# First batch's second attention stage: tokens on the PSUM partitions and PE transposes, in place of packed queries on the partitions and VectorE transposes

## The chip, the cores and the metric

The kernel runs on one core of a Trainium2 chip. The metric is the device time of one execution in microseconds (us), the median of several runs. A profiled execution of the kernel before is at hand: its span, its instructions by engine (PE is TensorE's matmuls, PEld its weight loads, DVE is VectorE, ACT is ScalarE, SP is SyncE, which issues most DMAs) and what each of them waited for.

## The reference: what is computed

Eight batches, eight heads of 64, 576 tokens. A set of 32 "packed" queries per head first attends to the tokens, and the tokens then attend to the 32 packed rows. An ELU feed-forward layer of width 2048 follows.

```
def sm_attn(qq, kk, vv):
    s = scale * np.matmul(qq, kk.transpose(0, 1, 3, 2))
    s = s - np.max(s, axis=-1, keepdims=True)
    a = np.exp(s)
    a = a / (np.sum(a, axis=-1, keepdims=True) + 1e-09)
    return np.matmul(a, vv)
p_packed = sm_attn(p, k, v)
out = sm_attn(q, p_packed, p_packed)
...
x = np.ascontiguousarray(attn_out.transpose(0, 2, 1, 3)).reshape(B * S, H * D)
h = x @ w_in
g = np.where(h > 0.0, h, alpha * (np.exp(np.minimum(h, 0.0)) - 1.0))
return (g @ w_out).astype(np.float32)
```

The weights arrive as 64-bit floats and are turned into 32-bit words on the chip.

## The kernel before, in words

**Stages.** For every batch, `attention` first lets the 32 packed queries of each head attend to all tokens: scores (`s1`, L476), maximum (`smax1`, L486), exponential (`sexp1`, L500), PE transposes of the exponentials (`tr1`, L531), the product with the values (`pv`, L557), its scaling by the sums (`norm`, L569), one more transpose (`tr2`, L583) and a copy that leaves the packed rows, heads stacked, in `ppT`. `mstep` multiplies these rows by w_in (L705), so that the up-projection later contracts over the 256 (head, packed row) pairs instead of 512 columns; its result `m_hi` is copied out by ScalarE. In the second stage the tokens attend to the packed rows: the scores of one half of the tokens (288) are made with the packed rows on the PSUM partitions (`s2`, L602: four heads' 32 rows in four strips of 32 partitions, two banks). The softmax runs over the 32 packed rows, so VectorE turns 32x32 blocks (`fold`, L610, one for each bank), and then takes the maximum (L617), the difference (L620), the sum (L630), the reciprocal (L633, L636) and the product (L639) along the free axis; ScalarE does the exponential (L626). VectorE turns the blocks back (`unfold`, L652) into `st.af`, where again the packed rows are on the partitions. For batches 0 and 1 the first quarter of the feed-forward layer reads `st.af` itself (L815, fp32); elsewhere a high and a low half are read (`a_hi` by a copy, `a_lo`, L658; L822).

**Feed-forward.** Each step of the order is a batch, a window of 256 or 320 of its tokens, and one of 16 blocks of the hidden width: up-projection (L815 or L822), relu and exponential on ScalarE (L829, L835), the ELU on VectorE (L838), and the down-projection (L932 fp32 for the first four blocks of batches 0 and 1, else L938, L939, L941). The first visits are batch 0's first window with blocks 0 to 3, its second window with the same blocks, then batch 1's.

**Weights.** `weights` turns each 128-wide block of w_in and w_out from 64-bit words into fp32 by four VectorE passes (L280, L295, L301, L308), a fifth that multiplies (L318) and two ScalarE passes (L287, L292). For w_out a high part (ScalarE, helper line L252) and a low part (VectorE, L331) are made beside.

**What sets the order.** A planner, `schedule`, takes all operations of the program with a priority and a planned cost for each engine and writes them out one by one. Each engine then works through its own list in that order: what stands behind a waiting instruction waits too. `T_ATT1`, `T_S2` and the like are priorities (a smaller one goes first), and a PSUM or SBUF buffer is given to an operation only when the planner sees it free. `temp()` hands batch 0 five buffers of its own.

Of the kernel before, what the change touches and what calls it, by code (L numbers as in the profile page):

```python
# [9 lines left out]
F32 = mybir.dt.float32  # L10
# [10 lines left out]
def packed_attention_elu_ffn(  # L21
# [58 lines left out]
    TM = [24.5, 24.5, 28.0, 28.0]  # L80
    T_S2, STAY, SWITCH = 0, 4, 0.12

    F_PLAIN, H_PLAIN = 4, [0, 1]
    T_WS, T_AS = 20, 6

# [160 lines left out]
    def ring_tile(ring, pool, shape, dt, tag, **kw):  # L248
        return Buf(R[ring], lambda: pool.tile(shape, dt, tag=tag, name=tag, **kw))
# [12 lines left out]
    def weights(f, first, prio):  # L262
# [71 lines left out]

        ld = op(-60 + f if first and f < 4 else -44 + f / 9 if f < 2 else prio - 8, {"DMA": 1.45}, load, take=[raw])
        x = op(prio, {"DVE": 0.42}, exponent, [ld], take=[ex_b], use=[raw])
# [32 lines left out]
    def attention(b, ts):  # L369

        st, prev_b = Batch(), sts.get(b - 1)
        p_b = ring_tile("p", small, [P, NPAIR, NPK], F32, "p")

# [15 lines left out]

        whole = b in H_PLAIN  # L390
        if whole:
# [18 lines left out]
        def queries(pair, half):  # L410
            if b == 0:
                return q_b[0].t[:, pair, half * HS:(half + 1) * HS]
            return q_b[half].t[:, :NPAIR * HS].rearrange("p (c s) -> p c s", c=NPAIR)[:, pair, :]

        def values(c, h):
# [30 lines left out]
        def load_q(e, n):  # L446
            if b == 0:
                nc.sync.dma_start(out=q_b[0].t, in_=qT[b])
            else:
                nc.sync.dma_start(  # L450
                    out=q_b[n].t[:, :NPAIR * HS].rearrange("p (c s) -> p c s", c=NPAIR),
                    in_=qT[b, :, :, n * HS:(n + 1) * HS],
                )

        lds, prev_ld = {}, prev_b and prev_b.ld_q
        for name, fn, bufs, t in (
            ("k", load_k, k_b, ts[0] - 6), ("v", load_v, v_b, ts[0] - 5), ("q", load_q, q_b, ts[0] - 3),
        ):
            lds[name] = []
            for n, x in enumerate(bufs):  # L460
# [130 lines left out]
        st.ppT_op = op(ts[3], {"ACT": 0.27, "DVE": 0.29}, tr2c, [o], use=[pt2, st.ppT])  # L591
        st.a_done, st.af_done = [], []
        prev = []
        for half in range(2):
            ps = banks(2)
# [19 lines left out]
            def smax(e, t3=t3, mx=mx):  # L615
                mx["t"] = small.tile([P, NB], F32, tag="mx2", name="mx2")
                nc.vector.tensor_reduce(out=mx["t"], in_=t3(), axis=AX.X, op=ALU.max)  # L617
# [10 lines left out]
            def ssum(e, t3=t3, sm=sm):  # L628
                sm["t"] = small.tile([P, NB], F32, tag="sm2", name="sm2")
                nc.vector.tensor_reduce(out=sm["t"], in_=t3(), axis=AX.X, op=ALU.add)  # L630
# [52 lines left out]
            )  # L683
            st.a_done.append(op(t, {"DVE": 0.75}, lo, [h], use=[t2, st.a]))
        st.tmp_last = prev[0]
        st.m, st.m_done = {}, {}
# [109 lines left out]
    for i, (b, win, f) in enumerate(order):  # L796
# [77 lines left out]
        a_b, a_done = (st.af, st.af_done) if h_whole else (st.a, st.a_done)  # L874
        need_a = a_done[0 if (b % 2, win) == (0, 0) else 1]
        cost = (1.07 if long else 0.87) if h_whole else (0.885 if long else 0.714)
# [138 lines left out]
```

## Time and profile before

| | |
|---|---|
| median of 3 runs | 725.19 us (724.35 to 727.75) |
| the profiled execution's own time | 724.5 us |
| its span | 722.3 us, so 2.2 us lie around it |
| PE matmuls, busy | 699.6 us, 97% |
| DVE, busy | 504.4 us, 70% |
| ACT, busy | 387.4 us, 54% |
| granted PE clock, mean | 0.998 |

Busy shares are averages over the whole span; the stage around the change is the first 40 us. A row of the chain of waits gives a start, a length and what ran; only the time by which a step moves the chain on is counted, so a step that overlaps its follower is shorter there than in the timeline, where each instruction has its full duration. One fp32 matmul of the program shows as two MATMUL rows. A matmul's shape gives the contraction and weight columns (64*32) and the moving operand (64x288).

### The profile page before, as it was taken

The numbers are of one execution on the slowest core, as the hardware profiler recorded it, in microseconds if no ns is written. First come the engines' busy times: TensorE is split into PE (matmuls) and PEld (weight loads), VectorE is DVE, ScalarE is ACT, GpSimd is POOL, SyncE is SP. The second block draws the span as 40 slices with busy tenths as digits, with TensorE's granted clock in tenths as the row PEclk, the third lists the DMA queues.
The fourth block names the chain that finished last, engine by engine and source line by source line (L and its number), as shares of the span: only waits on it lengthen the run. The fifth ranks groups of instructions, "written<-read, shape, count | busy, mean of one in ns | idle before, by whom it ended". The sixth has DMA issues, their size and how long they took to land.

```text
span 722.3 us, 13401 instructions
## 1 busy us (share of the span) xinstructions
PE 699.6 (97%) x5076; PEld 557.1 (77%) x5076; DVE 504.4 (70%) x1256; ACT 387.4 (54%) x900; POOL 19.4 (3%) x27
## 2 busy tenths in 40 slices
PE   2799999999999999999999999999999999999997
PEld 1454588887778877888878887888888877888886
DVE  6999998886875587545875569555686559654453
ACT  5777888885654455434454445434454345444332
POOL 0000002110111000000000000000000000000000
PEclk9999999999999999999999999999999999999999
DMA  9846546634543430003300250001400040000010
GB/s 348 296 150 204 186 147 142 132 66 108 165 59 44 123 108 1 30 1 128 117 2 29 67 165 1 2 29 66 160 21 1 30 132 30 1 30 1 0 45 30
DMA packets 29360, 61.42 MB, mean 85 GB/s; under 512 B 2544, under 2 KB 11760, under 8 KB 29040
## 3 DMA queue, kind: packets, MB, share of 16 engines
q1 hardware_dynamic: 26272, 55.06, 22.6%
q0 software_dynamic: 3024, 5.51, 5.6%
q8 instruction: 40, 0.66, 0.4%
q14 instruction: 24, 0.20, 0.1%
HBM read 45.61 MB, written 14.94 MB: 84 GB/s over the span
## 4 chain that ended last, share of the span: by engine, by line
PE 96%; DVE 1%; DMA 1%; ACT 1%; issue 0%; SPq 0%; ACTq 0%
PE psum L822 27%; PE psum L938 18%; PE psum L939 17%; PE psum L941 17%; PE psum L932 4%; PE psum L705 4%; PE psum L815 2%; PE psum L557 2%; PE psum L531 1%; PE psum L476 1%; PE psum L602 1%; DMA k<-in_kT 1%; DVE mx L486 0%; ACT tmp L500 0%; SPq L275 0%
## 5 line engine op out<-in xcount | busy, mean ns | idle before, releaser
L829 ACT ACTIVATE e<-psum 128x256 f32<-128x256 f32 (+1 forms) x256 | 105.4, 412 | 236.2 <-PE psum L822 214.4
L838 DVE SCALAR_TENSOR_TENSOR e<-e,psum 128x256 f32<-128x256 f32 (+1 forms) x240 | 103.6, 432 | 106.8 <-ACT e L835 106.1
L822 PE MATMUL psum<-a_hi,m_hi 128*128 128x256 f32 (+1 forms) x480 | 146.5, 305 | 0.0
L822 PE MATMUL psum<-a_lo,m_hi 128*128 128x256 f32 (+1 forms) x480 | 142.0, 296 | 0.0
L822 PE MATMUL psum<-a_hi,m_lo 128*128 128x256 f32 (+1 forms) x480 | 141.9, 296 | 0.0
L861 DVE TENSOR_TENSOR g_lo<-e,g_hi 128x256 fp32r<-128x256 f32 (+1 forms) x240 | 105.3, 439 | 22.0 <-ACT g_hi L252 7.1
L835 ACT ACTIVATE e<-e 128x256 f32<-128x256 f32 (+1 forms) x256 | 114.0, 445 | 6.1
L938 PE MATMUL psum<-wo_b,g_hi 128*128 128x512 f32 x288 | 114.8, 398 | 0.0
L939 PE MATMUL psum<-wo_b,g_hi 128*128 128x512 f32 x288 | 113.6, 394 | 0.0
L822 PEld LDWEIGHTS psum<-a_hi,m_hi 128*128 128x128 f32 x480 | 90.5, 189 | 24.2 <-issue 9.6
L938 PE MATMUL psum<-wo_a,g_hi 128*128 128x512 f32 x252 | 99.4, 394 | 0.0
L939 PE MATMUL psum<-wo_a,g_hi 128*128 128x512 f32 x252 | 99.3, 394 | 0.0
L822 PEld LDWEIGHTS psum<-a_lo,m_hi 128*128 128x128 f32 x480 | 90.7, 189 | 8.7 <-issue 1.0
L822 PEld LDWEIGHTS psum<-a_hi,m_lo 128*128 128x128 f32 x480 | 90.6, 189 | 0.0
L941 PE MATMUL psum<-wo_b,g_lo 128*128 128x512 f32 x288 | 86.6, 391 | 0.0
L941 PE MATMUL psum<-wo_a,g_lo 128*128 128x512 f32 x252 | 76.1, 392 | 0.0
L938 PEld LDWEIGHTS psum<-wo_b,g_hi 128*128 128x128 f32 x288 | 54.2, 188 | 12.1 <-issue 3.6
L941 PEld LDWEIGHTS psum<-wo_b,g_lo 128*128 128x128 f32 x288 | 54.1, 188 | 12.1
L252 DVE CAST g_hi<-e 128x256 fp32r<-128x256 f32 (+1 forms) x180 | 54.0, 300 | 12.5 <-PE psum L939 3.7
L939 PEld LDWEIGHTS psum<-wo_b,g_hi 128*128 128x128 f32 x288 | 54.3, 189 | 7.6
L941 PEld LDWEIGHTS psum<-wo_a,g_lo 128*128 128x128 f32 x252 | 47.3, 188 | 10.5
L938 PEld LDWEIGHTS psum<-wo_a,g_hi 128*128 128x128 f32 x252 | 47.5, 188 | 9.4 <-ACT g_hi L252 2.5
(88 smaller groups left out, 761.3 us busy)
## 6 DMA issues: line engine op xcount, KB each, us to landing
out<-part SPq DMA_DIRECT2D x36, 256.0 KB, 2.2
raw<-in_w_in SPq DMA_DIRECT2D x16, 512.0 KB, 3.7
kvq<-in_v SPq DMA_DIRECT2D x16, 512.0 KB, 5.1
raw<-in_w_out SPq DMA_DIRECT2D x16, 512.0 KB, 3.5
kvq<-in_kT SPq DMA_DIRECT2D x14, 576.0 KB, 4.5
kvq<-in_qT SPq DMA_DIRECT2D x14, 576.0 KB, 4.6
out<-part POOLq DMA_DIRECT2D x21, 256.0 KB, 4.4
k<-in_kT SPq DMA_DIRECT2D x1, 1152.0 KB, 7.4
```

Source lines behind the costliest of these rows:

```text
L252: (nc.scalar.copy if e == "ACT" else nc.vector.tensor_copy)(out=out, in_=in_)
L557: nc.tensor.matmul(ps.t[cols_of(pair), g, :D], lhsT=e1T[g].t[:n, c, cols_of(pair)], rhs=values(c, h)[:n], start=(c == 0), stop=(c == NKC - 1),
L705: nc.tensor.matmul(ps.t[cols_of(pair), g, :w], lhsT=st.ppT.t[rows_of(g), pair, :], rhs=w_in_sb[rows_of(g), pair, c * FC + part * w:c * FC ...
L822: nc.tensor.matmul(ps_b.t[:, :n_tok], lhsT=m_b[x].t[:, g, o:o + P], rhs=st.a.t[y][:, g, cols], start=(n == 0), stop=(n == 3 * G - 1),)
L829: nc.scalar.activation(out=e_b.t[:, :n_tok], in_=ps_b.t[:, :n_tok], func=AF.Relu, scale=-1.0)
L835: nc.scalar.activation(out=x, in_=x, func=AF.Exp, scale=-1.0)
L838: nc.vector.scalar_tensor_tensor(out=out, in0=e_b.t[:, cs], scalar=-1.0, in1=ps_b.t[:, cs], op0=ALU.add, op1=ALU.max)
L861: nc.vector.tensor_tensor(out=g_b.t[1][:, cs], in0=x, in1=g_b.t[0][:, cs].bitcast(F32), op=ALU.subtract)
L932: nc.tensor.matmul(a.t, lhsT=g_b.t[0][:, t].bitcast(F32), rhs=w_words[f // 2].t[:, f % 2, :], start=first, stop=final,)
L938: nc.tensor.matmul(a.t, lhsT=g_b.t[0][:, t], rhs=wo(f, 0), start=first, stop=False)
L939: nc.tensor.matmul(a.t, lhsT=g_b.t[0][:, t], rhs=wo(f, 1), start=False, stop=False)
L941: nc.tensor.matmul(a.t, lhsT=g_b.t[1][:, t], rhs=wo(f, 0), start=False, stop=final)
```

## The change

For batch 0 (`TOKENS = [0]`) `by_tokens` takes the place of `by_packs`, which is the old code and is kept for all other batches. It works by the windows of the feed-forward layer (256 and 320 tokens) instead of two halves of 288. In the scores' matmuls the operands trade places: 128 tokens' queries are the weights (64 x 128) and the packed rows move (64 x 32), so tokens lie on the PSUM partitions and the 32 packed rows of a head along the free axis. The 64 tokens that the second window has beyond 256 go into two strips of 64 partitions of one bank (`long`). Maximum and difference read PSUM directly, in one instruction for the two full blocks and one for the short one. After the product the probabilities are turned back by PE transposes into PSUM (`turn`) and copied to `st.af` (`put`, `put_half`; the planner may choose ScalarE or VectorE). `T_S2`, the priority of the second window's softmax, goes from 0 to -3. The list `FIRST` writes out the order of the first loads.

```
-    T_S2, STAY, SWITCH = 0, 4, 0.12
+    FIRST = "i0 i1 i2 i3 k v o0 o1 q".split()
+    T_S2, STAY, SWITCH = -3, 4, 0.12
...
+    TOKENS = [0]
...
+        def queries_of(pair, win, toks):
+            if b == 0:
+                return q_b[0].t[:, pair, toks]
...
-        for half in range(2):
+        def by_packs(half, prev):
...
+        def by_tokens(win, prev):
+            w = WINDOWS[b % 2][win]
+            n_tok = w.stop - w.start
+            long = n_tok > 2 * P
...
+            full = [slice(t0 + j * P, t0 + (j + 1) * P) for j in range(2)]
+            W = G * 2 * P
+            ng = (W + P * long) // NPK
+            ps, pt, t1 = banks(2), banks(2), temp()
...
+            def s2(e):
+                for j, toks in enumerate(full):
+                    for pair in range(NPAIR):
+                        for g in range(G):
+                            nc.tensor.matmul(
+                                ps.t[:, g, j * P + pair * NPK:j * P + (pair + 1) * NPK],
+                                lhsT=queries_of(pair, win, toks)[rows_of(g)],
+                                rhs=st.ppT.t[rows_of(g), pair, :], start=True, stop=True,
+                            )
+                if long:
+                    for pair in range(NPAIR):
+                        for g in range(G):
+                            o = 2 * P + pair * NPK
+                            nc.tensor.matmul(
+                                ps.t[rows_of(g), 0, o:o + NPK],
+                                lhsT=queries_of(pair, win, slice(t_half, t_half + HT))[rows_of(g)],
+                                rhs=st.ppT.t[rows_of(g), pair, :], start=True, stop=True,
+                            )
...
+            def smax(e):
+                mx["t"] = small.tile([P, NB + 2], F32, tag="mx2", name="mx2")
+                nc.vector.tensor_reduce(
+                    out=mx["t"][:, :W // NPK].rearrange("p (g n) -> p g n", g=G),
+                    in_=ps.t[:, :, :2 * P].rearrange("p g (n i) -> p g n i", i=NPK),
+                    axis=AX.X, op=ALU.max,
+                )
...
+            def turn(e):
+                for g in range(G):
+                    for j in range(2):
+                        o = (2 * g + j) * P
+                        nc.tensor.transpose(
+                            out=pt.t[:, g, j * P:(j + 1) * P], in_=flat1(o, o + P), identity=ident
+                        )
+                if long:
+                    nc.tensor.transpose(
+                        out=pt.t[:, 0, 2 * P:3 * P], in_=flat1(W, W + P), identity=ident
+                    )
+
+            def put(e):
+                copy(e, st.af.t[:, :G, t0:t0 + 2 * P], pt.t[:, :, :2 * P])
...
+            o = op(t, {"PE": 2.2 if long else 1.8}, s2, [qd[win % len(qd)], st.ppT_op],
+                   take=[ps], use=[q_b[win % len(qd)], st.ppT], mode=3)
+            s = op(t, {"DVE": 0.72}, smax, [o] + prev, use=[ps])
+            if long:
+                h = op(t, {"DVE": 0.27}, smax_half, [o], use=[ps], after=[s])
+            o = op(t, {"DVE": 0.72}, ssub, [s], take=[t1], use=[ps])
...
+            o = op(t, {"PE": 0.5}, turn, [o], take=[pt], use=[t1])
+            prev = [o]
+            o = op(t, {"ACT": 0.6, "DVE": 0.69}, put, [o], take=[] if win else [st.af],
+                   use=[pt] + [st.af] * win)
+            if long:
+                o = op(t, {"ACT": 0.27, "DVE": 0.3}, put_half, [o], use=[pt, st.af])
...
+        for half in range(2):
+            prev = (by_tokens if b in TOKENS else by_packs)(half, prev)
...
+        need_a = a_done[win if b in TOKENS else 0 if (b % 2, win) == (0, 0) else 1]
```

**What the planner makes of it.** Three places are shown; the line numbers of the changed kernel are higher than before. First PE's list, from the transpose that makes `ppT` for batch 0 on. Before (L602 the scores of a half, L705 the product with w_in, L476 batch 1's first scores):

```order
L583 MATMUL psum<-ident,pp 128x128
L602 MATMUL psum<-q_201,ppT 32x288 x8
L705 MATMUL psum<-w_in_sb,ppT 32x256 x8
L602 MATMUL psum<-q_201,ppT 32x288 x8
L705 MATMUL psum<-w_in_sb,ppT 32x256 x8
L476 MATMUL psum<-kvq,p 32x288 x16
```

Now (L724 and L733 the token scores, L878 the product with w_in, L495 batch 1's first scores, L550 its transposes, L799 `turn`):

```order
L602 MATMUL psum<-ident,pp 128x128
L724 MATMUL psum<-ppT,q_201 128x32 x32
L733 MATMUL psum<-ppT,q_201 64x32 x8
L878 MATMUL psum<-w_in_sb,ppT 32x256 x8
L495 MATMUL psum<-kvq,p 32x288 x16
L878 MATMUL psum<-w_in_sb,ppT 32x256 x8
L550 MATMUL psum<-ident,tmp 128x128 x4
L550 MATMUL psum<-ident,tmp 64x128
L799 MATMUL psum<-ident,tmp 128x128 x4
```

Both windows' scores, 40 matmuls, now stand ahead of batch 1's first scores, where 16 stood, and the first `turn` stands between the two groups of batch 1's transposes.

Second, PE's list from the first up-projection on. Before (L815 up-projection, L557 batch 1's `pv`, L583 its `tr2`, L932 down-projection):

```order
L815 MATMUL psum<-k_400,m_hi 128x256 x4
L557 MATMUL psum<-kvq,tmp 32x64 x40
L815 MATMUL psum<-k_400,m_hi 128x256 x2
L583 MATMUL psum<-ident,pp 128x128
L932 MATMUL psum<-w_words,g_hi 128x512 x2
```

Now (L988 up-projection, L576 `pv`, L602 `tr2`, L878 batch 1's product with w_in, L799 and L803 the second window's `turn`, L620 batch 1's scores, L1106 down-projection):

```order
L988 MATMUL psum<-k_430,m_hi 128x256 x4
L576 MATMUL psum<-kvq,tmp 32x64 x40
L602 MATMUL psum<-ident,pp 128x128
L878 MATMUL psum<-w_in_sb,ppT 32x256 x8
L799 MATMUL psum<-ident,tmp 128x128 x4
L803 MATMUL psum<-ident,tmp 128x128
L988 MATMUL psum<-k_430,m_hi 128x256 x4
L620 MATMUL psum<-kvq,ppT 32x288 x8
L1106 MATMUL psum<-w_words,g_hi 128x512 x2
```

The up-projection of blocks 2 and 3 stands behind the second window's `turn` now, and the first down-projection behind both.

Third, VectorE's list at the first softmax of batch 0. Before (L617 maximum, L620 difference, L630 sum, L486 batch 1's first maxima, L633 and L636 reciprocal, L639 product; the others are weights):

```order
L617 TENSOR_REDUCE mx_339<-tmp 128x18
L301 SCALAR_TENSOR_TENSOR mi<-raw,mi 128x512
L620 TENSOR_TENSOR tmp<-tmp,mx_339 128x576
L308 TENSOR_TENSOR ex<-ex,sg 128x512
L331 TENSOR_TENSOR wo_a<-w_words,wo_a 128x512
L630 TENSOR_REDUCE sm_370<-tmp 128x18
L486 TENSOR_REDUCE mx<-psum 128x1
L633 TENSOR_SCALAR sm_370<-sm_370 128x18
L636 RECIPROCAL sm_370<-sm_370 128x18
```

Now (L748 maximum, L763 difference, L782 sum, L505 batch 1's first maximum, L786 and L787 reciprocal):

```order
L748 TENSOR_REDUCE mx_342<-psum 128x16
L304 SCALAR_TENSOR_TENSOR mi<-raw,mi 128x512
L763 TENSOR_TENSOR tmp<-psum,mx_342 128x512
L311 TENSOR_TENSOR ex<-ex,sg 128x512
L334 TENSOR_TENSOR wo_a<-w_words,wo_a 128x512
L782 TENSOR_REDUCE sm_383<-tmp 128x16
L505 TENSOR_REDUCE mx<-psum 128x1
L786 TENSOR_SCALAR sm_383<-sm_383 128x16
L787 RECIPROCAL sm_383<-sm_383 128x16
```

The two `fold`s that stood ahead are gone and one more L334 stands there; the steps' succession is the same, with batch 1's maximum between sum and reciprocal as before. The planner gives `put` to ScalarE. SyncE's list keeps its order through batch 1's query loads.

More of the change, by code (lines that the diff above doesn't have):

```diff
@@ L333, in low @@
             )
-        ld = op(-60 + f if first and f < 4 else -44 + f / 9 if f < 2 else prio - 8, {"DMA": 1.45}, load, take=[raw])
+        name = ("i" if first else "o") + str(f)
+        t = FIRST.index(name) - 60 if name in FIRST else prio - 8
+        ld = op(t, {"DMA": 1.45}, load, take=[raw])
         x = op(prio, {"DVE": 0.42}, exponent, [ld], take=[ex_b], use=[raw])
@@ L371, in attention @@
         st, prev_b = Batch(), sts.get(b - 1)
+        whole = b in H_PLAIN
         p_b = ring_tile("p", small, [P, NPAIR, NPK], F32, "p")
@@ L387, in attention @@
         ))
-        whole = b in H_PLAIN
         if whole:
@@ L413, in queries @@
             return q_b[half].t[:, :NPAIR * HS].rearrange("p (c s) -> p c s", c=NPAIR)[:, pair, :]
+        def queries_of(pair, win, toks):
+            if b == 0:
+                return q_b[0].t[:, pair, toks]
+            w = WINDOWS[b % 2][win]
+            n = w.stop - w.start
+            x = q_b[win].t[:, :NPAIR * n].rearrange("p (c s) -> p c s", c=NPAIR)[:, pair, :]
+            return x[:, toks.start - w.start:toks.stop - w.start]
         def values(c, h):
@@ L449, in load_q @@
             else:
+                w = WINDOWS[b % 2][n] if b in TOKENS else slice(n * HS, (n + 1) * HS)
                 nc.sync.dma_start(
-                    out=q_b[n].t[:, :NPAIR * HS].rearrange("p (c s) -> p c s", c=NPAIR),
-                    in_=qT[b, :, :, n * HS:(n + 1) * HS],
+                    out=q_b[n].t[:, :NPAIR * (w.stop - w.start)].rearrange(
+                        "p (c s) -> p c s", c=NPAIR
+                    ),
+                    in_=qT[b, :, :, w],
                 )
@@ L459, in attention @@
             lds[name] = []
+            if b == 0:
+                t = FIRST.index(name) - 60
             for n, x in enumerate(bufs):
@@ L685, in attention @@
+        st.a_done, st.af_done = [], []
+        prev = []
+        for half in range(2):
+            prev = (by_tokens if b in TOKENS else by_packs)(half, prev)
         st.tmp_last = prev[0]
```

78 lines of the change are left out of this document (73 added, 5 removed).

## The prediction

> **What bounds the kernel now.** I read the page first, then the stages, then the chain of waits through the first 40 us, since that is where batch 0's second attention stage runs. The page gives the chain that ended last by engine:
>
> ```profile
> PE 96%; DVE 1%; DMA 1%; ACT 1%; issue 0%; SPq 0%; ACTq 0%
> ```
>
> TensorE is the bound: 96% of the chain is PE. A change that lies in the first 40 us can therefore pay only by letting PE start its unbroken work earlier, or by taking work out of it. Busy time by stage (engines with instruction counts, then granted PE clock, DMA share and rate) shows where PE is not full:
>
> ```profile
> 10.00:20.00 10.00, 6.97 (x122) 4.77 (x122) 8.92 (x22) 6.11 (x13) 0.00 (x0) 1.00 1.03 396
> 20.00:30.00 10.00, 5.53 (x114) 2.41 (x103) 9.20 (x21) 6.86 (x15) 0.00 (x0) 1.00 0.96 347
> 30.00:40.00 10.00, 9.35 (x109) 6.76 (x108) 9.00 (x22) 8.05 (x21) 0.00 (x0) 0.83 0.64 203
> 40.00:50.00 10.00, 10.00 (x73) 4.80 (x72) 9.46 (x24) 6.92 (x15) 0.00 (x0) 1.00 0.31 102
> ```
>
> PE is half busy or a little more to 30 us, and full from 40 us on. VectorE is about 90% busy from 10 us on, so it leads at the start. The chain of waits (start, time it moves the chain on, what ran) says which steps, from the first `fold` (L610) to the first down-projections:
>
> ```profile
> 22.35 0.40 DVE tmp L610
> 22.75 0.33 DVE ex L280
> ...
> 23.46 0.31 DVE mi L295
> 23.77 0.66 DVE mx L617
> 24.43 0.60 DVE mi L301
> 25.03 0.67 DVE tmp L620
> 25.70 0.34 DVE ex L308
> 26.03 0.60 DVE wo_a L331
> 26.63 0.66 DVE sm L630
> 27.30 0.67 DVE mx L486
> 27.96 0.09 DVE sm L633
> ...
> 28.08 0.27 DVE sm L636
> 28.36 0.66 DVE mx L486
> ...
> 34.63 1.39 PE psum L557 x80
> 36.02 1.06 PE psum L815 x4
> ...
> 37.12 0.33 PE psum L583
> 37.45 1.72 PE psum L932 x4
> 39.16 0.86 PE psum L815 x4
> ```
>
> The softmax of batch 0's first half goes down VectorE's list step by step, with the weights' passes and batch 1's maxima (L486) between. From the first up-projection on PE goes from row to row with hardly a gap. PE's and ScalarE's own rows in that stretch (start, duration, engine, what) give the durations for the sum:
>
> ```profile
> 21.38 0.72 PE L602 MATMUL psum<-q,ppT 64*32 64x288 f32 x16 [0.38 <-ACT ppT L252]
> ...
> 25.23 1.67 PE L476 MATMUL psum<-kvq,p 64*32 64x288 f32 x32 [1.05 <-ACT m_hi L252]
> ...
> 25.72 0.64 PEld L476 LDWEIGHTS psum<-kvq,p 64*32 64x32 f32 x24 [0.34 <-DMA kvq<-in_kT]
> 25.73 0.69 ACT L626 ACTIVATE tmp<-tmp 128x576 f32<-128x576 f32 x1 [0.56 <-DVE tmp L620]
> ...
> 29.35 0.50 PEld L531 LDWEIGHTS psum<-ident,tmp 128*128 128x128 f32 x5 [2.99 <-ACT tmp L500]
> ...
> 29.84 0.74 ACT L500 ACTIVATE tmp<-psum,nb 128x576 f32<-128x576 f32 x1 [0.55 <-DVE nb L494]
> ...
> 30.58 0.57 ACT L252 COPY tmp<-psum 128x512 f32<-128x512 f32 x1
> ...
> 31.85 2.78 PE L815 MATMUL psum<-k,m_hi 128*128 128x256 f32 x8
> ...
> 37.82 0.26 ACT L252 COPY ppT<-psum 128x128 f32<-128x128 f32 x1
> ```
>
> The first up-projection (L815) runs from 31.85 us.
>
> **What leaves VectorE.** The groups of VectorE's instructions by shape, from 20 to 100 us (count, busy us and mean ns):
>
> ```profile
> L610 DVE STREAM_TRANSPOSE tmp<-psum 128x288 f32<-128x288 f32 x8 | 3.8, 472 | 0.2 <-PE psum L602 0.2
> ...
> L652 DVE STREAM_TRANSPOSE k<-tmp 128x576 f32<-128x576 f32 x2 | 1.5, 772 | 0.0
> ...
> L838 DVE SCALAR_TENSOR_TENSOR half_sb<-e,psum 128x64 f32<-128x64 f32 x7 | 1.5, 208 | 0.3 <-ACT e L835 0.3
> ```
>
> Batch 0 loses four `fold`s, 4 x 0.472 = 1.9 us, and two `unfold`s, 2 x 0.772 = 1.5 us. The other passes cover 512 + 640 columns in place of 2 x 576, the same number. The short block's own maximum and difference are new; the nearest row is the 64-column one at 0.21 us, so 0.2 us each. VectorE is lighter by 3.0 us. ScalarE gets two `put`s like its 512-column copy, 0.57 us each, and a short one; it has room (8.05 of 10 us busy at most). No DMA moves: SyncE's list keeps its order through batch 1's query loads.
>
> **The token scores, the term that matters.** Out go the two L602 groups, whose rows at 21.38 us and later are 0.7 us each. In come 32 + 8 matmuls; those of 128 tokens have 128 weight columns where L602 had 32. The trace has no matmul of 64 x 128 weights, so I bound it. In units of one load of 128 columns there are 32 x 2 + 8 x 2 / 2 = 72 (two rows for each fp32 matmul; the short block's 64 columns count half).
>
> High end: the transposes' loads at 29.35 us, five of up to 128 columns in 0.50 us, 0.10 us each; 72 of them one after the other are 7.2 us. Low end: batch 1's `pv`, 80 pairs of load and matmul in 1.39 us, hence 1.4 us if columns cost nothing. Taken by its columns, 32 each, the same row gives 1.39 / 80 x 4 = 0.070 us for 128 columns and 72 x 0.070 = 5.0 us. Between them is the question whether the two halves of the array (heads' rows 0 to 63 and 64 to 127, which alternate here) work side by side. In the chain's rows for batch 1's scores and for the product with w_in they do:
>
> ```profile
> 41.74 1.13 PE psum L602 x32
> ...
> 45.23 0.59 PE psum L705 x16
> ```
>
> 32 rows of 288 columns in 1.13 us are 35 ns each, while one such row alone would stream for about the time of a 512-column one times 288/512, 1.72 / 4 x 288 / 512 = 0.24 us; seven run at once, of eight that could. Side by side, 7.2 us become 3.6. I take 4.3 us, the mean of 3.6 and 5.0, and keep 1.4 and 7.2 for the range.
>
> A rule of the Trainium skill speaks against the change. TensorE: Matmul & The Clock Gate, section "LDWEIGHTS (loading the stationary operand)", has a load cost by its columns alone, about 107 ns for 128, whatever the contraction depth; by that 72 loads would be an estimated 7.7 us. The 0.10 us row agrees with the figure for a single load. The Trainium skill's page TensorEngine Tiling (Array Packing), section "Key Properties", lets different tiles load and multiply in parallel, which would halve it; no row here shows that for 128 columns.
>
> **Where it falls.** PE has idle time here, so the scores cost nothing as PE work; they cost because batch 1's scores (L476, 1.67 us) now stand behind all 40 of them, and batch 1's first maximum stands on VectorE ahead of batch 0's reciprocal and product. Step by step, with the chain's lengths (512 columns 0.60 us, as L301 and L331):
>
> PE: token scores from 21.38 to 25.7 us (the first window done at 23.3), product with w_in 0.59, 26.3, batch 1's scores 1.67, 28.0 us. Before they ended at 26.9; their load, awaited to 25.72 us, sets no later start.
>
> VectorE from 22.35 us, where the first `fold` began: low part 0.60, two weight passes 0.33 and 0.31, maximum 0.60 (its scores are there since 23.3), pass 0.60, difference 0.60, pass 0.34, low part 0.60, 26.35; sum 0.60 (the exponential, 0.69 on ScalarE, is done by 26.2), 26.95. Then it waits until 28.0, a wait of 1.05 us that is new. Maximum 0.67, reciprocal 0.09 + 0.27, maximum 0.66, product 0.60: 30.3 us. Then `turn`, four transposes of 0.10, 30.7; `put` stands behind batch 1's second exponential on ScalarE (0.74 us from about 30.5), so it runs from 31.2 to 31.8 us. The first up-projection starts at 31.8 where it started at 31.85. The 0.8 us of two `fold`s (0.40 each) and the 0.77 of `unfold` are spent on the low part, the wait, `turn` and `put`.
>
> The second window goes on down VectorE: 30.5 + weights 0.60 and 0.33, maximum 0.60 + 0.20, difference 0.60 + 0.20, batch 1's reciprocal 0.36 as the other, weights 0.31, 0.33 and 0.60, sum 0.73, weights 0.34, reciprocal 0.36, weights 0.60, product 0.73 (640 columns by 0.66 for 576): 37.4 us.
>
> PE from 31.8 us: two blocks of up-projection, 1.72 us at full clock; before they took 2.78, because the clock was down just then:
>
> ```profile
> 30.00:32.00 2.00, 1.39 (x8) 1.24 (x7) 1.97 (x7) 1.97 (x6) 0.00 (x0) 0.55 0.97 355
> ```
>
> It follows 2.4 us without PE work (26.9 to 29.35). Now `turn` and later scores shorten that hole to about 1 us, so the drop may or may not come; I carry both, 33.5 or 34.4 us. `pv` 1.39: 34.9 or 35.8. From its end to `tr2` it was 36.02 to 37.12, 1.1 us, for the scaling on ScalarE, and 0.96 us more until `ppT` was copied (37.82 + 0.26). Before, block 2's up-projection and the first down-projections filled this; now PE's list has nothing but `tr2`, batch 1's product with w_in (0.59) and the second `turn`. So the product starts at 37.0 or 37.85 and ends at 37.6 or 38.45, VectorE's 37.4 is no later, and the second `turn`, five transposes, 0.5 us, ends at 38.1 or 38.95 us. From here PE is full in both kernels.
>
> What PE has behind it there, compared: before, by 38.1 us, block 2 (0.86) and 0.65 us of down-projection beyond the common part, against 0.59 of product now: 0.9 us behind. By 38.95 us, 0.86 + 1.50 - 0.59 = 1.8 behind. The middle is **1.3 us lost**. What VectorE saves later can win little, as this is PE's only idle row from 40 to 80 us (in brackets the idle time and its releaser):
>
> ```profile
> 64.22 1.34 PE L815 MATMUL psum<-q,m_hi 128*128 128x320 f32 x4 [0.15 <-DVE g_hi L838]
> ```
>
> So 724.5 + 1.3 = 725.8 us for a profiled execution; the median of the runs shown lies 0.7 above the profiled one, and I say 726.1 us.
>
> **Rivals.** *Loads one after the other* (the slower side). The place is PE's list between `tr2` and batch 1's scores. At 7.2 us those scores end at 30.9, and everything from VectorE's first wait shifts by 2.9 us: 1.3 + 2.9 = 4.2 lost, 728.7 us. It decides against the change from about 6.6 us of token scores on (3.6 us lost). For it speaks the 0.10 us row, against it the seven at once. By the figure of the Trainium skill's page TensorE: Matmul & The Clock Gate (section on LDWEIGHTS) an estimated 4.7 us would be lost, 729.2 us.
>
> *VectorE's relief comes through.* If the scores take 3.4 us or less, batch 1's scores wait for their load again, VectorE's wait shrinks from 1.05 to about 0.4, and the first up-projection starts about 0.6 us early; with the drop of the clock avoided (0.9 lost instead of 1.3) and the 0.15 us saved later: 0.9 - 0.6 - 0.15 = 0.15 lost, 724.7 us. Were VectorE's wait to vanish wholly, the gain would be 0.3 us, 724.2. For it speaks that VectorE leads to 32 us; against it, that each step saved meets another engine's wait, and that PE is full from 40 us on.
>
> *A later wait.* After the second `turn` PE does blocks 2 and 3, 1.72 us, to 39.8 or 40.7 us, and then batch 1's scores, whose queries are loaded once `pv` has freed their buffer. The page's issues have the median time to landing as the last column:
>
> ```profile
> kvq<-in_qT SPq DMA_DIRECT2D x14, 576.0 KB, 4.6
> ```
>
> From `pv`'s end that is 39.5 or 40.4 us, 0.3 us in time. A landing 1 us later would cost 0.7 us: 726.5 us.
>
> **Numbers.** About 0.5%, 3.6 us, is what can be told from no change. Forecast with the later wait 0.58, serial loads 0.22, relief 0.20. Slower by over 3.6 us: most of the serial case (0.13) and 0.08 of the forecast, where a wait has been missed: 0.21. Faster by over 3.6 us: no row gives that, so 0.07 for what I have missed. The rest, 0.72, is no change. The range goes from 722.5 (relief, with the runs' spread of a microsecond or two) to 730 (serial loads with the clock down).
>
> **What would show it.** Right: token scores of about 4 us in PE's rows from 21.4; VectorE idle about 1 us before batch 1's first maximum; the first up-projection within 0.5 us of 31.8; PE idle 1 to 2 us between `pv` and the second `turn`; nothing different after 70 us. Wrong: token scores over 6.6 or under 3 us; an up-projection before 31 us; a PE gap after 45 us, or a shift of the end that PE's idle time in the first 40 us doesn't account for.

## The result, and the profile after

The changed kernel takes 731.83 us (median, 730.20 to 732.90) where the kernel before, run beside it, takes 725.43 us (724.35 to 728.76). The ratio is 1.007, with a 95% interval of 1.0047 to 1.0093: slower, with an interval that leaves out no change and begins just under the prediction's 0.5%. The forecast was 726.1 us, and 730 us was the end of its range. Of the seven executions, the three with a mean granted clock of 0.993 or 0.994 took 730.2 to 730.5 us and the four with 0.999 or 1.0, the profiled one among them, 731.8 to 732.9 us, so a mean of 1.0 is no sign of a faster TensorE. The profiled execution took 732.33 us, with a span of 730.1 us, 7.8 us longer than the span of 722.3 us before.

The page's busy time by engine, kernel after:

```profile
PE 708.5 (97%) x5133; PEld 566.5 (78%) x5133; DVE 502.8 (69%) x1256; ACT 388.6 (53%) x899; POOL 19.4 (3%) x27
```

TensorE was busy for 699.6 us before and is busy for 708.5 us now, 8.9 us more. Outside its busy time it has 21.6 us of the span, where it had 22.7. So the loss is in the main no new waiting of TensorE: its work has become longer. Busy time by stage in the kernel after (PE, PEld, DVE, ACT and POOL with instruction counts, then the granted clock, the share of DMA and its rate):

```profile
20.00:30.00 10.00, 9.19 (x105) 8.37 (x105) 6.24 (x12) 4.31 (x9) 0.00 (x0) 1.00 0.83 308
```

In the stage from 20 to 30 us TensorE was half busy (5.53 of 10 us) and VectorE led with 9.20; now TensorE has 9.19 and VectorE 6.24. The two have changed places.

How the loss grows shows in up-projection rows further on, the same rows in both timelines. The kernel before:

```profile
151.36 0.28 PE L822 MATMUL psum<-a_hi,m_hi 128*128 128x256 f32 x1
...
209.63 0.28 PE L822 MATMUL psum<-a_hi,m_hi 128*128 128x256 f32 x1
```

The changed kernel, with the last batch's packed scores (L620):

```profile
157.68 0.28 PE L995 MATMUL psum<-a_hi,m_hi 128*128 128x256 f32 x1
...
216.67 0.28 PE L995 MATMUL psum<-a_hi,m_hi 128*128 128x256 f32 x1
...
601.56 0.72 PE L620 MATMUL psum<-kvq,ppT 64*32 64x288 f32 x16 [0.66 <-DMA kvq<-in_qT]
```

The changed kernel is 6.3 us behind at 151 us and 7.0 us behind at 210 us. Between these rows TensorE has no idle time over 0.1 us in either kernel, but the planner gave its rows another order. At 601 us it waits 0.66 us for the last batch's queries, where the kernel before doesn't wait, and from there it is 7.8 us behind. So 6.3 us of this pair's loss belong to the first stages, and 1.4 us come long after them. Whether the change causes the wait at 601 us is not shown: run e10 below, with TensorE's rows in the same order there, doesn't have it.

The chain of waits of the kernel after, from the token scores to the first up-projection. L724 and L733 are the token scores, L878 the product with w_in, L495 batch 1's first scores, L550 the transposes of its exponentials, L799 `turn`, L988 the up-projection:

```profile
21.48 7.04 PE psum L724 x64
28.52 0.99 PE psum L733 x16
29.51 1.03 PE psum L878 x16
30.55 1.92 PE psum L495 x32
...
34.80 1.33 PE psum L550 x5
36.13 0.85 PE psum L799 x4
36.98 0.97 PE psum L550 x5
37.95 1.73 PE psum L988 x8
```

Where the chain ran down VectorE's list before, it is now one row of TensorE's after the other. The token scores take 7.04 + 0.99 = 8.03 us, 0.110 us for each of the 64 long rows. The rows behind them are slow as well: the product with w_in takes 1.03 us, where the row of before quoted in the prediction has 0.59 for the same 16 instructions. The timeline of the same stretch gives the idle time ahead of an instruction, in brackets with its releaser:

```profile
25.15 0.69 DVE L748 TENSOR_REDUCE mx<-psum 128x16 f32<-128x512 f32 x1 [1.55 <-PE psum L724]
...
32.58 0.76 DVE L505 TENSOR_REDUCE mx<-psum 128x1 f32<-128x576 f32 x1 [4.01 <-PE psum L495]
...
37.79 1.89 PE L988 MATMUL psum<-k,m_hi 128*128 128x256 f32 x8
...
41.90 0.33 PE L602 MATMUL psum<-ident,pp 128*128 128x128 f32 x1 [0.83 <-ACT pp L588]
42.58 0.67 PE L878 MATMUL psum<-w_in_sb,ppT 64*32 64x256 f32 x16 [0.35 <-ACT ppT L255]
```

VectorE waits 1.55 us for the first window's scores and 4.01 us ahead of batch 1's first maximum. The first up-projection starts at 37.79 us, where the timeline of before has 31.85.

The half speed does not stand in the clock column, which has 1.00 for 20 to 40 us here. It is read from the durations. The column counts only the stretches at half rate of which the trace has a record. The first change of the clock that the changed kernel's trace records is a rise to full rate at 37.72 us; the kernel before has that rise at 19.98 us already, and half rate from 30.22 to 33.63 us. So the durations and the records together say that TensorE had not come to full rate when the token scores began, and did not until they were done. Whether the clock makes the 8.03 us is the first question of the experiments.

### The profile page after: what moved, and what is told of

The parts are those of the page before. It is cut to its first block, busy times and chain, and to the rows that moved or that the text cites. A ratio compares the mean times of both kernels' runs of the same rounds, so it can differ in the third digit from the quotient of the medians.

```text
span 730.1 us, 13532 instructions
## 1 busy us (share of the span) xinstructions
PE 708.5 (97%) x5133; PEld 566.5 (78%) x5133; DVE 502.8 (69%) x1256; ACT 388.6 (53%) x899; POOL 19.4 (3%) x27
## 4 chain that ended last, share of the span: by engine, by line
PE 96%; DMA 2%; ACT 1%; DVE 0%; issue 0%; SPq 0%
PE psum L995 27%; PE psum L1112 17%; PE psum L1113 17%; PE psum L1115 17%; PE psum L878 5%; PE psum L1106 4%; PE psum L988 2%; PE psum L576 2%; PE psum L550 2%; PE psum L495 2%; PE psum L620 1%; DMA k<-in_kT 1%; PE psum L724 1%; DMA kvq<-in_qT 1%; ACT tmp L519 0%
```

## The experiments

Two theories explain 8.03 us. **Loads one after the other**: 72 loads of 128 columns at 0.10 to 0.11 us don't overlap between the array's halves (the rival of the prediction). **The clock**: the halves do work side by side, at about 0.055 us a row, but the rows run at half the clock.

### e1_rates: the token form by itself

A kernel of its own, which computes rates only and leaves out the attention and the feed-forward layer. Each form follows a stretch of 512-column matmuls, but for the first, and has eight rows of 128 x 256 (a probe) behind it:

```
+for n in range(64):
+    nc.tensor.matmul(out=ps[:, g, ...32 columns],              # g = n % 2, or always 0
+                     lhsT=q[64 * g:64 * g + 64, pair, 128 tokens], rhs=p[64 * g:64 * g + 64, pair, :])
```

> A measurement of the disputed cost by itself: only the first batch's q and p are loaded, no attention and no feed-forward is done and the output is zeros. PE does runs of 64 matmuls: token form (64 x 128 weights, 32 columns moving, heads' halves alternating) first from an idle PE, then after 17 us of 512-column matmuls; then all on one half of the array; then 128 x 128 transposes; then packed form (64 x 32 weights, 256 columns moving); then token form with all 128 rows; then token form with one 512-column matmul in every five. Four 256-column matmuls behind each run show the clock. Theory A (loads one after the other, whatever the clock): 0.110 us for each of the 128 rows, alternating or not, cold or warm. Theory B (the clock is the cause: the rows ran at half clock): 0.110 us from idle, 0.055 to 0.06 us after the long matmuls, at least for the first 3 us of the run, and with long matmuls between throughout; the probe behind the run at 0.43 us a row if the run let the clock drop, 0.215 if not. If the halves of the array worked side by side, one half alone would take up to twice as long.

The chain of waits of this kernel (start, length, what; 64 matmuls are 128 rows). L49 is the token form without a warm-up (its probe is left out here), L55 after one, L61 on one half of the array only, L67 transposes of 128 x 128, L74 the packed form (32 weight columns, 256 moving); L57, L69 and L79 are probes:

```profile
31.10 13.87 PE ps L49 x128
...
66.11 10.63 PE ps L55 x128
76.73 3.45 PE ps L57 x8
...
97.35 24.75 PE ps L61 x128
...
143.92 6.99 PE ps L67 x64
150.91 1.73 PE ps L69 x8
...
169.80 3.61 PE ps L74 x128
173.42 1.92 PE ps L79 x8
```

The windows within the second token stretch:

```profile
68.00:69.00 1.00, 1.00 (x24) 1.00 (x22) 0.00 (x0) 0.00 (x0) 1.00 0.06 16
69.00:70.00 1.00, 1.00 (x20) 1.00 (x18) 0.00 (x0) 0.00 (x0) 0.78 0.00 0
70.00:71.00 1.00, 1.00 (x13) 1.00 (x12) 0.00 (x0) 0.00 (x0) 0.50 0.00 0
```

One half of the array alone takes 24.75 us for its 128 rows, both in turn 13.87. The two stretches are not at the same clock throughout: the one-half stretch begins at full clock and comes to 0.50 at 101 us. At the same clock, by the starts of its rows, one half takes 0.213 us a row and both take 0.106 at half clock, 0.112 and 0.057 at full clock: the halves work side by side, and the first theory falls. The same form over all 128 rows of the array (L83, not shown) takes 24.00 us, about as long as one half alone, and loses the clock too. The stretch after the warm-up begins at full clock and loses it between 69 and 70 us, about 3.5 us after its start, although the profile has TensorE busy for every microsecond. With x rows at 0.054 us and the others at the 0.108 us (13.87 / 128) of the stretch without a warm-up, 0.054 x + 0.108 (128 - x) = 10.63 gives x = 59, or 3.2 us of full speed. Its probe then takes 3.45 us, twice the 1.73 us behind the transposes, which hold the clock at about the same 0.109 us a row; the packed form holds it too, at 0.028 us. So of the three forms it is the token form, 32 columns moving for each load of 128 columns, that lets the clock fall.

The Trainium skill's page TensorE: Matmul & The Clock Gate, section "Part 1: The HAM clock gate (the "warmup" mystery)", has a free-running window of some 3.4 us after which an idle array is put at half rate. The length agrees with the 3.2 to 3.5 us here. That the array must be idle does not agree with 1.00 us busy in each of these windows: by these rows, TensorE busy in the profile is not enough to hold the clock.

### e2_ts2: the priority alone

```
-    T_S2, STAY, SWITCH = -3, 4, 0.12
+    T_S2, STAY, SWITCH = 0, 4, 0.12
```

> The changed kernel with the second window's priority back at 0. Both theories on the token scores (A and B): within 1 us of the changed kernel, 731 to 733 us, as PE's list is the same up to the second turn. Theory C (the new priority makes the hole before the second turn): 2 us or more come back, 729 us.

731.87 us, ratio 1.0097 (1.0079 to 1.0115): nothing comes back, so the changed priority by itself is no cause.

### e3_behind: the place in TensorE's list

The second window's token scores stand behind batch 1's first scores.

```
+        if b == 1:
+            prev_b.s2_op.after.append(o1)
```

> The changed kernel, with the second window's token scores held until batch 1's first scores are written, so 16 matmuls in place of 40 stand ahead of these. Theory A with its place (it is the delay of batch 1's scores that costs): these end at about 28 us in place of 32.5, the first up-projection starts at 34 to 35 us in place of 38, and 2 to 3.5 us come back: 728 to 730 us. If the place does not matter, only PE's total work: 731.8 us as before.

732.56 us, ratio 1.0107 (1.0081 to 1.0133): nothing came back. Its chain (L726 are token scores, L991 the up-projection):

```profile
28.07 1.92 PE psum L495 x32
29.99 3.55 PE psum L726 x32
...
37.71 2.10 PE psum L991 x8
```

Batch 1's scores end at 29.99 us, 2.5 us earlier than in the changed kernel, and the up-projection starts at 37.71, 0.24 us earlier. The prediction had the loss in whoever stands behind the token scores. That is not so: TensorE itself is late by then, and its list has the same work in any order.

### e4_delay: the kernel before with the delay alone

36 unread token matmuls (72 rows) ahead of batch 1's first scores in the kernel before.

```
+                for n in range(36 if b == 0 and half else 0):
+                    nc.tensor.matmul(ps.t[:, n % 2, HS:HS + NPK], lhsT=...128 tokens, rhs=...32 packed rows)
```

> The kernel before, with its old scores and VectorE transposes, and 36 token-form matmuls (whose results nobody reads) put ahead of batch 1's first scores. Theory A with its place: 72 rows of 0.110 us, 7.9 us, let batch 1's scores end at 34 to 35 us in place of 26.9, and 4 to 7 us are lost: 729.5 to 732.5 us, so the delay alone makes most of the loss of the change. If the loss comes from turn, put and the hole behind them, under 2 us are lost here: below 727.5 us.

731.74 us (728.14 to 735.86), ratio 1.008 (1.0051 to 1.0109). By the medians, these rows alone, without any other part of the change, cost about as much as the whole change. The four executions are far apart, and the other parts of the change may still win and lose about the same. The chain:

```profile
24.54 7.82 PE psum L609 x72
32.36 1.12 PE psum L711 x16
```

Here too they run at 0.109 us a row, and the product with w_in behind them at 1.12.

### e5_both: batch 1 in the same way

```
-    TOKENS = [0]
+    TOKENS = [0, 1]
```

> The changed kernel with batch 1 in token form too: the cost doubled, and the second time where PE has hardly any idle time. There the long matmuls between keep the clock up; 80 rows at 0.055 to 0.11 us are 4.4 to 8.8 us against 1.1 us of packed scores, and nine transposes are 0.9: if PE's time is the price, 4 to 8 us more are lost, 736 to 740 us; if the loss was only in the start's waits, under 2 us more, 734 us at most.

738.49 us, ratio 1.0177 (1.0146 to 1.0209), 6.7 us above the changed kernel's median, as expected if TensorE's time is the price. Batch 1's scores come when TensorE has been busy with long matmuls:

```profile
43.96 1.98 PE psum L724 x32
45.93 0.58 PE psum L733 x16
46.52 2.69 PE psum L724 x32
49.21 3.71 PE psum L1106 x4
52.92 1.80 PE psum L988 x4
54.72 1.72 PE psum L1106 x4
56.44 1.08 PE psum L988 x4
```

The first 32 rows take 0.062 us each, the later 0.084, and then four down-projection rows take 3.71 us where the same four take 1.72 a little later. This is e1's fall of the clock inside the kernel, and the trace records half rate from 47.43 to 54.25 us: about 5 us of token scores slow down long matmuls that have nothing to do with them, by 2.0 + 0.7 us.

### e6 and e7: filler matmuls, too long

If the clock at 21 us is the cause, keeping TensorE busy before should help. e6 adds fillers to the kernel before, e7 the same to the changed kernel: 12 matmuls of 512 columns ahead of the very first scores and 5 of 224 columns behind the scores of batches 0 and 1.

```
+            if b == 0:
+                wide(12, ps1[0].t[:, 0, :], 512)
...
+            if b < 2:
+                wide(5, ps1[0].t[:, 0, HS:], 512 - HS)
```

> The kernel before, with matmuls on a constant tile, whose results nobody reads, where PE waits at the start: 12 of 512 columns ahead of batch 0's first scores (PE waits for k until 10.1 us there), and 5 of 224 columns behind the first scores of batches 0 and 1. No work is left out. Theory B (the clock): PE's first rows run at full clock, so the first scores take about 1.2 us in place of 2.27, the first transposes 1.1 in place of 2.17, the first product with the values 1.2 in place of 2.13, and the drop at 30 us does not come; 2 to 4 us are won: 721 to 723.5 us. If the clock at the start costs nothing (other waits end those steps): 725 us, within 1 us.

> The changed kernel with the same idle-time matmuls. Theory B: the token scores begin at full clock, so about 60 of the 80 rows go at 0.055 us and the rest at 0.11 (5 to 6 us in place of 8), and the first rows gain as in the kernel before: 4 to 6 us come back, 726 to 728 us, so that the distance to the kernel before with the same matmuls shrinks from 6.4 to 4 us or less. If the loads alone set the price: rows of 0.110 us from the first one, and the distance stays at 6 us or more.

e6 takes 732.82 us, ratio 1.0103 (1.0080 to 1.0126), and e7 739.81 us, ratio 1.0197 (1.0170 to 1.0224). Neither shows the gain that was expected, since the filler was mis-sized:

```profile
2.21 12.47 PE psum L475 x24
14.69 1.13 PE psum L486 x32
```

The 24 rows (chain of e6) take 12.47 us, so the first scores (L486) wait for them instead of for their data. Then they take 1.13 us, where the chain of the kernel before has 2.27 from 10.15 us on. The clock matters as thought, but the price was higher than the gain. In e7 the 64 long rows took 7.04 us again: the last filler ahead of them ends at 17.4 us, 8 us before them, and the trace records half rate from 22.10 us on.

### e8 and e9: a short filler

Five matmuls of 512 columns, while TensorE waits for the first keys anyway. e8 is the kernel before with them, e9 the changed kernel.

```
+            for _ in range(5 if b == 0 else 0):
+                nc.tensor.matmul(ps1[0].t[:, 0, :], lhsT=wide_sb[:, :P], rhs=wide_sb, start=True, stop=True)
```

> The kernel before, with only 5 matmuls of 512 columns on a constant tile ahead of batch 0's first scores, while PE waits for k (10 rows at 0.43 us at full clock, 0.86 at half: 6 to 8.6 us from 2.2 us on, done before 10.1). No work is left out. Theory B (the clock): the first scores take 1.13 us in place of 2.27, and the transposes behind them may keep the full clock: 1 to 3 us won, 722 to 724.2 us, faster than both kernels. If other waits end those steps: 724.6 us, unchanged.

> The changed kernel with the same 5 matmuls. Theory B, as worked out from the rates measured by themselves: the first scores win 1.1 us; the token scores come 11 us later, so that the clock has been at half again or falls within 3.4 us of them: rows of 0.110 us for most of the 80, and 729.5 to 731 us. The distance to the kernel before with the same matmuls stays about 6 us.

e8 takes 724.55 us, ratio 0.9985 (0.9972 to 0.9998), the lowest median of all variants here. The 1 to 3 us expected did not come. The 0.15% lie far below the 0.5% named in the prediction, and the interval just leaves out 1, so it is a small gain at best. In its timeline the first scores take half of what they did:

```profile
10.05 1.20 PE L482 MATMUL psum<-k,p 64*32 64x288 f32 x32 [2.18 <-DMA k<-in_kT]
```

e9 takes 731.14 us, ratio 1.0080 (1.0060 to 1.0099): no measurable gain. But here the clock column does show the low clock. First a window of e9, then its timeline, where L730 and L739 are the token scores and L884 the product with w_in:

```profile
26.00:29.00 3.00, 3.00 (x57) 1.74 (x61) 0.89 (x2) 1.11 (x3) 0.00 (x0) 0.50 0.65 251
```

```profile
20.38 5.41 PE L730 MATMUL psum<-ppT,q 64*128 64x32 f32 x64 [0.38 <-ACT ppT L257]
25.71 1.06 PE L739 MATMUL psum<-ppT,q 64*64 64x32 f32 x16
26.70 1.10 PE L884 MATMUL psum<-w_in_sb,ppT 64*32 64x256 f32 x16
```

The short block takes 1.06 us and the product with w_in 1.10 us at a granted clock of 0.50. In the changed kernel the two are 1.06 and 1.10 us in the timeline as well (0.99 and 1.03 in its chain), so that kernel ran them at half clock, whatever its column says. The 64 long rows took 7.04 us in the changed kernel, 6.23 in e2, 5.41 here and 4.97 in e5. By the traces' records the clock falls 0.9 us after the first of these rows in e2, 1.8 in e9 and 2.3 in e5, and in the changed kernel it was down from the first row: where in such a stretch the clock falls differs.

### e10_bf16: the same scores, short

The token scores from the upper 16 bits of both operands as bf16, one row for each matmul. The scores' low bits are left out.

```
+            def top(x):
+                return x.bitcast(BF16).rearrange("p (n t) -> p n t", t=2)[:, :, 1]
...
-                                lhsT=queries_of(pair, win, toks)[rows_of(g)],
-                                rhs=st.ppT.t[rows_of(g), pair, :], start=True, stop=True,
+                                lhsT=top(queries_of(pair, win, toks)[rows_of(g)]),
+                                rhs=top(st.ppT.t[rows_of(g), pair, :]), start=True, stop=True,
```

> The changed kernel with its token scores' matmuls on the upper 16 bits of queries and packed rows, read as bf16 where they lie: one row in place of two for each matmul. The scores' low bits are left out; all else is as in the changed kernel. Theory B and the sum of the prediction (scores of 3.4 us or less make batch 1's scores wait for their load again, and the change about even): scores of 2.2 us or less at full clock, 4.4 at half, first up-projection at 31 to 33 us, 724.5 to 727 us. If turn, put and the hole behind the second turn cost by themselves: still 728 us or more.

727.69 us (726.12 to 731.24), ratio 1.0039 (1.0023 to 1.0054), between the two ranges expected. The timeline has the 40 rows, 1.0 us in place of 8.03, a wait of batch 1's first scores (L495) for their keys, and the idle time that is left behind `pv` and ahead of batch 1's packed scores:

```profile
21.59 0.61 PE L727 MATMUL psum<-ppT,q 64*128 64x32 bf16 x32 [0.35 <-ACT ppT L255]
22.13 0.40 PE L736 MATMUL psum<-ppT,q 64*64 64x32 bf16 x8
...
28.28 1.66 PE L495 MATMUL psum<-kvq,p 64*32 64x288 f32 x20 [1.53 <-DMA kvq<-in_kT]
...
38.81 0.33 PE L602 MATMUL psum<-ident,pp 128*128 128x128 f32 x1 [0.83 <-ACT pp L588]
39.49 0.67 PE L881 MATMUL psum<-w_in_sb,ppT 64*32 64x256 f32 x16 [0.35 <-ACT ppT L255]
...
43.22 0.72 PE L620 MATMUL psum<-kvq,ppT 64*32 64x288 f32 x16 [0.64 <-DMA kvq<-in_qT]
```

By the medians, 4.1 us of the 6.4 us come back with the length of the scores; by the ratios, whose intervals overlap a little, 2.2 of 5.1. Some 2.4 us stay above the kernel before. The three idle times from 38.81 us on are 1.8 us, but in this execution (729.04 us) 2.0 us are lost by the end of `pv` already, which comes at 37.98 us and came at 36.02.

### e11 and e12: other work in that idle time

With `T_S2 = 2` the planner puts up- and down-projections between `pv` and the second `turn`. e11 is the changed kernel with that, e12 is e10 with it (low bits of the scores left out, as there).

```
-    T_S2, STAY, SWITCH = -3, 4, 0.12
+    T_S2, STAY, SWITCH = 2, 4, 0.12
```

> The changed kernel with the second window's softmax at priority 2. On TensorE the second window's token scores then stand behind the product with w_in, and blocks 2's up-projections and the first down-projection stand between pv and the second turn, where the changed kernel has about 1.3 to 2 us of idle time. If that hole carries the part of the loss that the token scores' duration does not: 1 to 2 us back, 730 to 731 us. If TensorE's total of slow rows alone sets the start: no change, 731.8 us, with the hole gone and the same time lost elsewhere.

> The kernel with the token scores in bf16 (low bits of the scores left out) and the same priority 2. The run with bf16 alone gave 727.7 us, 2.4 us above the kernel before. If the idle time behind pv is that rest, 725.5 to 726.5 us; if the rest is the planner's other order or a later load, 727 us or more.

e12 takes 726.43 us, ratio 1.0003 (0.9988 to 1.0019), level with the kernel before. Its timeline in the same place (L1109 is the down-projection):

```profile
38.27 1.88 PE L1109 MATMUL psum<-w_words,g_hi 128*128 128x512 f32 x4
39.99 0.27 PE L602 MATMUL psum<-ident,pp 128*128 128x128 f32 x1
```

No bracket is left ahead of L602. The intervals of e10 and e12 don't overlap; the difference of the ratios, 0.0036, is 2.6 us, the rest that e10 had left. So with short scores the planner's other order brings that rest back. Whether it does so by filling the idle time behind `pv` is not separated here: the first up-projection starts earlier as well, at 32.60 us where e10 has 34.59.

In e11, with the slow scores, the same order brought nothing: 731.73 us, ratio 1.0075 (1.0050 to 1.0099). Why the filled idle time pays only where the scores are short isn't settled.

## Why the prediction was wrong, point by point

**What bounds the kernel.** Right that most is decided in the first 40 us. Wrong that nothing differs after 70 us: 1.4 us of the 7.8 us by which the span grew came after 151 us, from rows in another order and from the wait at 601 us, and neither has a term in the sum. Wrong above all in "PE has idle time here, so the scores cost nothing as PE work". That was meant for 4 us of scores; with 8 us TensorE has 9.19 of 10 us and is the bound, which fits e3, where another order of the same work brought nothing back.

**The token scores, the term that failed.** Taken at 4.3 us, they measured 8.03, at half clock. The question put to the trace, whether the two halves work side by side, was answered rightly: 0.213 us a row on one half, 0.106 on both, at the same clock. At full clock 4.3 us was a fair size: e5's warm rows give 64 x 0.062 + 0.58 = 4.5 us. What the step left out is that every duration of the sum supposes a clock. The profile of before had the warnings. One is the 0.55 at 30 to 32 us, which the prediction used as a drop that "may or may not come" for the up-projection, not for the rows that it was adding. The other is batch 0's first scores, 2.27 us at 10.15 us in the chain for 32 rows that take 1.13 at 41.74: TensorE starts at half rate, whatever the column says.

**The rival of serial loads** came nearest, 728.7 us or 729.2, by a mechanism that isn't there. 72 loads of 0.10 us are 7.2 us, and half of them at half clock are 7.2 us as well; one number can't tell them apart. The rival's point of 6.6 us, from which the change is slower, was passed, and it was slower.

**The walk behind them.** It had the product with w_in at 0.59 us and batch 1's scores at 1.67; they took 1.03 and 1.92. With the scores at 8.03 us the walk's own steps would give the up-projection at about 31.8 + 3.7 = 35.5 us. It came at 37.79. The 2.3 us between are these slower rows (0.44 + 0.25 = 0.7) and TensorE's own list ahead of the up-projection: ten transposes of batch 1 and `turn` take 1.33 + 0.85 + 0.97 = 3.15 us there, where the walk had 0.4 for `turn` and 1.1 until `put` was done, since it took TensorE to be free (1.65 more). Against it, the up-projection took 1.89 us in the timeline and not the 2.78 of before, as the walk's "two blocks at full clock" had it.

**VectorE.** A new wait of 1.05 us ahead of batch 1's first maximum was predicted, 4.01 us came, in the right place. VectorE was to be 3.0 us lighter and is 504.4 - 502.8 = 1.6 us lighter by the page; which of its passes made the difference wasn't followed, since VectorE led nowhere any more. The rival of its relief needed scores of 3.4 us or less. e10 and e12 have about 1.0 us of them. In e10 batch 1's first scores do wait for their load again, as that rival had it, but until 28.28 us and not 25.72; and e12 is level with the kernel before, so even then the relief brought no time that shows.

**The idle time behind `pv`** was predicted at 1 to 2 us; 0.83 + 0.35 us stand in the timeline. **The later wait** did not come: batch 1's packed scores start at 45.76 us with no wait over 0.1 us, in time as the walk had it. The only wait for queries in the changed kernel is the last batch's, 0.66 us at 601 us, which no term foresaw.

**The sum with the sizes measured**, from the profiled executions: the up-projection starts 5.9 us later and is done 5.0 us later. The 5.9 us are, to 0.1, the 3.7 of the scores themselves and the 2.3 of the walk behind them. With the second `turn` and the idle time behind `pv` the distance is 6.3 us at 151 us, where the walk's own steps gave 0.9 us for all that follows the up-projection's start at full clock and 0.4 came. The other order adds 0.7 by 210 us and the wait at 601 us 0.7 more: 7.8 us, rounding apart.

**The chances.** Slower had 0.21, for the serial loads and missed waits. No share was given to a low clock in the scores by itself, though the profile of before showed a low clock in that stage; only the end of the range was set by "serial loads with the clock down".

## What to carry to other kernels

Trading a matmul's operands so that 128 columns are loaded for 32 that move makes each row cost about its load: at full clock 0.112 us on one half of the array with 32 columns moving, and 0.109 for a transpose with 128. Such rows can also let the clock fall to half, 0.9 to 3.5 us after the first of them in these runs, for themselves and for the long matmuls behind them. So a duration that is carried to another place in the program needs the clock at both places beside it, read from a row of known full-clock length where the clock column is silent. And before a cost is called hidden because an engine has idle time, the same sum should be made with the cost doubled: here that would have turned the hidden engine into the bound.

## What the runs showed of the hardware that was not expected

- A stretch of token-form matmuls with TensorE busy by the profile for every microsecond lost the clock after about 3.5 us (e1: 1.00, 0.78, 0.50). Transposes of 128 columns with the same 0.11 us a row did not.
- Kept apart by long matmuls, the token form doesn't lose it. In e1's last stretch, four token matmuls stand between single 512-column ones, and eight rows still take 0.57 us, 0.071 each, some 15 us into the stretch (chain of e1):

```profile
252.59 0.57 PE ps L94 x8
```

- The clock column can read 1.00 while the rows run at half speed: 1.10 us for the product with w_in at a column of 1.00 in the changed kernel, and at 0.50 in e9. In the changed kernel that is the time ahead of the first change on record, the rise at 37.72 us.
